# Attention scores as 64-row matmuls in couples on the two halves of TensorE's rows

## The chip, the cores and the metric

The kernel runs on one core of a Trainium2 chip. The metric is the device time of one execution in microseconds, the median of three runs. Five engines work side by side, each through its own queue in order: TensorE (PE in the profile, with its weight loads listed apart as PEld), VectorE (DVE), ScalarE (ACT), GpSimd (POOL) and SyncE (SP, which here only issues DMAs).

## The reference, cut to what matters

Attention with normed queries and keys, then a low-rank mixer and a two-layer MLP:

```python
# q, k, v: (8, 12, 448, 64); U: (448, 32); V: (32, 448); w_ch1: (768, 3072); w_ch2: (3072, 768)
q_n, k_n = rmsnorm(q, g_q), rmsnorm(k, g_k)            # over the 64 values of a head
scores = 0.125 * q_n @ k_n.transpose(0, 1, 3, 2)       # 448 x 448 for each head
attn = softmax(scores) ; a = attn @ v                  # heads side by side: x (8, 448, 768)
u = x + ((x.transpose(0, 2, 1) @ U) @ V).transpose(0, 2, 1)
out = u + np.maximum(u @ w_ch1, 0.0) @ w_ch2
```

A head is 64 wide, half of the 128 rows over which a full matmul of TensorE sums. 448 keys are three and a half blocks of 128.

## The kernel before

**Groups and pairs.** The 96 heads (8 batches of 12) are worked in 48 pairs, six to a batch, and loaded in 24 groups of two pairs. For a pair, `qT` holds 128 rows by 448 tokens: head 0 in rows 0 to 63, head 1 in rows 64 to 127, with the gains multiplied in.

**Keys, `kz`.** For a pair there are 128 rows by 896 columns: the 448 keys of head 0 stand in rows 0 to 63 with zeros below them, then the 448 keys of head 1 in rows 64 to 127 with zeros above them. So each block of 128 columns can be multiplied with all of `qT`, and the zeros drop the wrong head. Seven blocks make up a pair: three of head 0, a shared one with the last 64 keys of both heads, three of head 1. For the first six groups the keys are turned by TensorE (`turn`) and copied into `kz` by VectorE (`take_k`, L359 to L361). From group 6 on (`DMA_FROM`) GpSimd scales them into `kp` (`scale_dma`, L188 and L192), 14 blocks of 128 with the zeros in place, and SyncE's transposing DMAs bring them into `kz` (`turn_dma`, L367 and L369); then GpSimd multiplies the gains into `qT` (`take_dma`, L374).

**Scores, `Sc(b, pr, r)`.** For r = 0 to 2 two matmuls (L398) of 128 x 448 go into the two banks of a tile `sc` (pool `ps_sc`, two tiles), and one exponential on ScalarE (L399) takes both to the tile `E`, 128 x 896. For r = 3 there is one matmul and an exponential half as long.

**Values, `V(b, pr, half)`.** 14 matmuls (L412 and L416) read `E` as weights and write a tile `pv` of the pool `ps`, which has four tiles of one bank each and serves everything else too; two operations of VectorE finish them. The first matmul of each seven reads the block of last keys.

**Mixer and MLP.** For each batch: `mix_t`, `mix_tr`, `mix_rows` (L433, L440, L485), 24 `up` (six matmuls of 128 x 448 at L500, then a Relu on ScalarE, L502), and `down` (L526: units of six matmuls of 128 x 384).

**The order.** It is written out by hand (`manual_schedule`). Two lists are merged by a planner: `att`, the attention steps, each with a cost, and `mlp`, the units of mixer and MLP. A step of `att` is taken as long as its costs so far are not ahead of what is due beside the MLP. Batch 0 runs before the MLP, in an order of its own (`extra`). From batch 1 on, the four `Sc` of a pair are four steps, with the two `V` of the pair before, the turns (`T`), the squares and sums of later groups, and the loads between them. Since attention runs ahead (`LEAD`), it ends well before the MLP does.

Of the kernel before, what the change touches and what calls it, by code (L numbers as in the profile page):

```python
# [9 lines left out]
FP32 = mybir.dt.float32  # L10
BF16 = mybir.dt.bfloat16
# [8 lines left out]
DMA_FROM = 6  # L20
# [4 lines left out]
def kernel(  # L25
# [13 lines left out]
    nc = tc.nc  # L39
# [43 lines left out]
    va_bufs = [consts.tile([P, NM, D1], BF16, name=f"va{i}") for i in range(3)]  # L83
    vl_bufs = [consts.tile([P, 2, 2 * D1], BF16, name=f"vl{i}") for i in range(3)]

    kp = consts.tile([P, 2 * NT, P], BF16)
    q_bufs = [consts.tile([P, 2, S], BF16, name=f"qT{i}") for i in range(2)]
    kz_bufs = [consts.tile([P, 2, 2 * S], BF16, name=f"kz{i}") for i in range(2)]

    def load_qk(gi, i, eng=None):  # L90
        b, h0, n = groups[gi]
# [84 lines left out]
    def scale_dma(gi, i):  # L176

        src = staged[gi][i].rearrange("p (c j) d -> p c j d", c=2)
        rs = rss[gi][:, i].rearrange("p (c j) -> p c j ()", c=2)
        for c in range(2):  # L180
            if i == 0:
                dst = normed[gi][0][:, :, c]
                odd = groups[gi][0] % 2
                main, rest = dst[:, odd:odd + 2 * NJ], dst[:, (1 - odd) * 2 * NJ]
            else:
                dst = normed[gi][1].rearrange("p (c j) (x d) -> p c j x d", c=2, x=2)[:, c, :, c]
                main, rest = dst[:, c:c + 2 * NJ], dst[:, (1 - c) * 2 * NJ]
            nc.gpsimd.tensor_tensor(  # L188
                main.rearrange("p (t i) d -> p i t d", i=2),
                src[:, c, :2 * NJ].rearrange("p (i t) d -> p i t d", i=2),  # L190
                rs[:, c, :2 * NJ].rearrange("p (i t) o -> p i t o", i=2).to_broadcast([P, 2, NJ, D]), ALU.mult)
            nc.gpsimd.tensor_tensor(rest, src[:, c, 2 * NJ], rs[:, c, 2 * NJ].to_broadcast([P, D]), ALU.mult)  # L192
# [49 lines left out]
    for va, vl in zip(va_bufs, vl_bufs):  # L242
        nc.vector.memset(va[:, :, D:D1], 1.0)
        nc.vector.memset(vl, 0.0)
        for e in range(2):
            nc.vector.memset(vl[e * R:(e + 1) * R, :, e * D1 + D:(e + 1) * D1], 1.0)
    for t, eng in zip(kz_bufs, (nc.vector, nc.gpsimd)):
        for a in range(2):
            eng.memset(t[D:P, a, :S], 0.0)
            eng.memset(t[0:D, a, S:], 0.0)  # L250
    for e in range(2):
        nc.gpsimd.tensor_mul(gp[:, e * D:(e + 1) * D], grow[:, 0, :], grow[:, 1, :])

# [101 lines left out]

    def take_k(gi, a):
        src = pts[(gi, 1)][:, :, a, :]
        kz = kz_bufs[gi % 2][:, a]
        nc.vector.tensor_copy(kz[0:D, :S].rearrange("p (j r) -> p j r", r=R), src[0:D])  # L359
        nc.vector.tensor_copy(kz[D:P, S:S + R], src[D:P, 2 * NJ])  # L360
        nc.vector.tensor_copy(kz[D:P, S + R:].rearrange("p (j r) -> p j r", r=R), src[D:P, :2 * NJ])  # L361
        qk[(gi, a)].append(kz)

    def turn_dma(gi):
        for a in range(2):
            rows = slice(a * R, (a + 1) * R)
            nc.sync.dma_start_transpose(q_bufs[gi % 2][:, a].rearrange("p (j r) -> p j r", r=R),  # L367
                                        normed[gi][0][rows].rearrange("p j c d -> p (j c d)"))
            nc.sync.dma_start_transpose(kz_bufs[gi % 2][:, a].rearrange("p (g r) -> p g r", r=R),  # L369
                                        kp[rows].rearrange("p g x -> p (g x)"))  # L370

    def take_dma(gi):
        qT = q_bufs[gi % 2]
        nc.gpsimd.tensor_scalar(qT, qT, gg[:, 0:1], None, ALU.mult)  # L374
        for a in range(2):
            qk[(gi, a)] = [qT[:, a], kz_bufs[gi % 2][:, a]]

    def T(gi, i):
        if gi >= DMA_FROM:
# [8 lines left out]
    NB = 2 * NJ + 1  # L388

    def Sc(b, pr, r):  # L390
        qT, kz = qk[divmod(b * NPAIR + pr, 2)]
        if r == 0:
            es[(b, pr)] = ep.tile([P, NB, S], BF16, name="E", tag="E")
        n = min(2, NB - 2 * r)
        sc = ps_sc.tile([P, 2, 512], FP32, name="sc", tag="sc")
        for i in range(n):
            c = (2 * r + i) * P
            nc.tensor.matmul(sc[:, i, :S], kz[:, c:c + P], qT, start=True, stop=True)  # L398
        nc.scalar.activation(es[(b, pr)][:, 2 * r:2 * r + n, :], sc[:, :n, :S], AF.Exp, scale=scal, bias=bias)  # L399

    def V(b, pr, half):
        if b not in xs:
            xs[b] = xp.tile([P, NW, dm], BF16, name="x", tag="x")
        gi, lp = divmod(b * NPAIR + pr, 2)
        va, vl = normed[gi][2:]
        first_h, step = (2 * lp, 1) if gi == BESIDE else (lp, 2)
        h0 = groups[gi][1] + first_h
        E = es[(b, pr)]
        pv = ps.tile([P, 2, 2, D1], FP32, name="pv", tag="ps")
        for i in range(2):  # L410
            w = WIN[b % 2][2 * half + i]
            nc.tensor.matmul(pv[:, i].rearrange("p e d -> p (e d)"), E[:, NJ, w:w + P], vl[:, lp, :],  # L412
                             start=True, stop=False)
            for e in range(2):
                for j in range(NJ):
                    nc.tensor.matmul(pv[:, i, e, :], E[:, e * (NJ + 1) + j, w:w + P],  # L416
                                     va[:, (first_h + step * e) * NJ + j, :], start=False, stop=(e == 1 and j == NJ - 1))
        r = headp.tile([P, 2, 2], FP32, name="r", tag="r")
        nc.vector.reciprocal(r, pv[:, :, :, D])  # L419
        nc.vector.tensor_tensor(  # L420
            xs[b].rearrange("p i (h d) -> p i h d", d=D)[:, 2 * half:2 * half + 2, h0:h0 + step + 1:step, :],
            pv[:, :, :, :D],
            r.rearrange("p i e -> p i e ()").to_broadcast([P, 2, 2, D]), ALU.mult)
# [124 lines left out]
    def add_att(cost, f, *a):  # L548
        att.append((cost, f, a))
# [55 lines left out]
    for i, (b, pr) in enumerate(pairs):  # L605
        if b == 0:
            continue
        gi, a = divmod(i, 2)
        more = gi + 1 < len(groups)
        by_dma = gi + 1 >= DMA_FROM  # L610
        soon = gi + 2 < len(groups)

        if pr == 0 and b > 1:
            add_att(0.55, V, *pairs[i - 1], 0)
            add_att(0.55, V, *pairs[i - 1], 1)
        add_att(0.38, Sc, b, pr, 0)
        if i == 2 * DMA_FROM - 2:
            add_att(0.0, load, DMA_FROM + 1)
        if a == 0 and by_dma and gi + 1 < len(groups):
            add_att(0.0, scale_all, gi + 1)  # L620
        if b == 1 and pr == 0:
            add_att(0.4, lambda: None)
        if a == 0 and not by_dma:
            add_att(0.0, squares, gi + 1, 0, nc.gpsimd)
            add_att(0.0, squares, gi + 1, 1, nc.gpsimd)
            if gi + 2 >= DMA_FROM:
                add_att(0.0, load, gi + 2)
        add_att(0.38, Sc, b, pr, 1)
        if pr != 0:
            add_att(0.55, V, *pairs[i - 1], 0)  # L630
        if a == 1 and more and not by_dma:
            add_att(0.39, T, gi + 1, 0)
        if a == 1 and soon and gi + 2 >= DMA_FROM:
            add_att(0.0, squares, gi + 2, 0)
            add_att(0.0, squares, gi + 2, 1)
        add_att(0.38, Sc, b, pr, 2)
        if a == 0 and not by_dma:
            add_att(0.0, sums, gi + 1, 0)
            add_att(0.0, sums, gi + 1, 1)
        if a == 0 and more and by_dma:  # L640
            add_att(0.0, turn_dma, gi + 1)
            add_att(0.0, take_dma, gi + 1)
            if gi + 1 == DMA_FROM:
                add_att(0.0, weights, 2)
            if gi + 3 < len(groups):
                add_att(0.0, load, gi + 3)
        if a == 1 and more and not by_dma:
            add_att(0.39, T, gi + 1, 1)
        if a == 0 and not by_dma:
            add_att(0.0, scale_all, gi + 1)  # L650
        add_att(0.19, Sc, b, pr, 3)
        if pr != 0:
            add_att(0.55, V, *pairs[i - 1], 1)
        if a == 1 and soon and gi + 2 >= DMA_FROM:
            add_att(0.0, sums, gi + 2, 0)
            add_att(0.0, sums, gi + 2, 1)
    add_att(0.55, V, *pairs[-1], 0)
    add_att(0.55, V, *pairs[-1], 1)

# [93 lines left out]
    while ia < len(att) or im < len(mlp):  # L753
# [6 lines left out]
        if take_att:  # L760
            c, f, a = att[ia]
            if f is load:
                later.append((f, a))
            else:
                f(*a)
            if ia >= a_from:
                ca += c
            ia += 1
            if f is scale_all:
                weights(2)  # L770
            if f is T and a == (DMA_FROM - 1, 1):
                nc.vector.memset(kp, 0.0)
        else:
            c, f, a, _ = mlp[im]
            f(*a)
            turning = f is mix_t and a[0] > 0 or turning and a != (a[0], NW - 1, 1)
            cm += c
            im += 1
# [30 lines left out]
```

## Time and profile before

| What | Value |
|---|---|
| median of 3 runs (lowest, highest) | 601.6 us (601.02, 602.13) |
| span of the profiled execution | 600.9 us |
| around the span, to the median of the runs | 0.7 us |
| PE busy, share of the span | 585.0 us, 97% |
| ACT busy | 313.5 us, 52% |
| DVE busy / POOL busy | 200.2 us, 33% / 203.3 us, 34% |
| DMA | 71.73 MB, mean 119 GB/s |
| granted TensorE clock | full speed in all 40 slices |
| matmuls of the scores (L398) | 336, 93.9 us busy, mean 352 ns |
| exponentials (L399) | 144 of 896 columns, mean 1003 ns; 48 of 448, mean 635 ns |
| first and last matmul of the scores | 11.3 us, 486.3 us |

Matmuls overlap in the pipeline, so the mean of 352 ns is not what one of them costs in a row of many: twelve matmuls of 448 columns last 2.27 us. The page counts an engine as busy while anything of its is in flight; idle time is put down to the event that ended it. The first 44 us are batch 0, in which TensorE is busy 36.3 us; from 110 us to 470 us it is busy throughout.

### The profile page before, as it was taken

The page shows a single profiled execution, that of the slowest core. Times are in us where ns is not written, and L with a number is a line of the kernel's source. Part 1 is how long each engine was busy: PE and PEld are TensorE (multiplying, and loading weights), DVE is VectorE, ACT ScalarE, POOL GpSimd, SP SyncE. Part 2 cuts the span into 40 slices and gives each one's busy share as a digit, 9 for nine tenths or more (in the row PEclk, how much of TensorE's full clock was granted, in tenths as well). Part 3 has the DMA queues.
Part 4 walks back from the last instruction along what each step waited for, and adds up shares of the span by engine and source line. Part 5 has one row for each costly group of instructions (what it writes and reads, how often), then busy time and mean ns, then how long its engine had stood idle before and what let it go on. Part 6 is the DMA issues. An engine that isn't in the chain of part 4 may idle for free.

```text
span 600.9 us, 11614 instructions
## 1 busy us (share of the span) xinstructions
PE 585.0 (97%) x4791; PEld 356.1 (59%) x4792; DVE 200.2 (33%) x456; ACT 313.5 (52%) x482; POOL 203.3 (34%) x290
## 2 busy tenths in 40 slices
PE   8798999999999999999999999999999999999996
PEld 7464666655666556655566655665566655655563
DVE  6785544512334212531235320531233310310011
ACT  6866793467454776357654567356763344004300
POOL 6996655335054323425144413524233000000000
PEclk9999999999999999999999999999999999999999
DMA  8899999685279451973275742677026310230022
GB/s 224 201 240 239 259 180 215 127 199 100 85 150 161 127 131 32 193 178 82 58 164 100 188 116 41 151 180 169 9 38 100 74 27 0 53 74 1 0 53 52
DMA packets 118332, 71.73 MB, mean 119 GB/s; under 512 B 80392, under 2 KB 115080, under 8 KB 118280
## 3 DMA queue, kind: packets, MB, share of 16 engines
q1 hardware_dynamic: 108868, 61.56, 45.5%
q0 software_dynamic: 9408, 9.44, 9.7%
q8 instruction: 37, 0.61, 0.4%
q14 instruction: 15, 0.12, 0.1%
q10 hardware_dynamic: 4, 0.00, 0.0%
HBM read 52.20 MB, written 11.01 MB: 105 GB/s over the span
## 4 chain that ended last, share of the span: by engine, by line
PE 90%; DMA 4%; DVE 2%; ACT 1%; issue 0%; POOL 0%; SPq 0%; DVEq 0%; ACTq 0%
PE ph L500 36%; PE po L526 34%; PE sc L398 9%; PE pv L416 5%; DMA kz<-kp 2%; PE pv L412 2%; DMA kf<-in_k_dram 2%; PE pm L485 1%; ACT E L399 1%; DMA out_dram<-ob 1%; PE pu L433 1%; DVE ssq L159 1%; PE pt L344 0%; PE sc L512 0%; POOL kp L169 0%
## 5 line engine op out<-in xcount | busy, mean ns | idle before, releaser
L526 PE MATMUL po<-w2b,hT 128*128 128x384 bf16 x1344 | 241.8, 326 | 0.0
L500 PE MATMUL ph<-uT,w1b 128*128 128x448 bf16 x1140 | 234.4, 352 | 0.0
L399 ACT ACTIVATE E<-sc,gg 128x896 bf16<-128x896 f32 x192 | 172.5, 911 | 112.7 <-PE sc L398 112.5
L526 PEld LDWEIGHTS <-hT 128*128 128x128 bf16 x1344 | 126.7, 98 | 78.8
L502 ACT ACTIVATE hT<-ph 128x448 bf16<-128x448 f32 x190 | 102.9, 544 | 121.2 <-PE ph L500 118.9
L500 PEld LDWEIGHTS <-w1b 128*128 128x128 bf16 x1140 | 108.2, 97 | 95.4
L398 PE MATMUL sc<-qT,kz 128*128 128x448 bf16 x336 | 93.9, 352 | 7.7 <-ACT E L399 5.9
L419 DVE RECIPROCAL r<-pv 128x4 f32<-128x4 f32 x96 | 17.4, 181 | 210.7 <-PE pv L416 209.9
L188 POOL TENSOR_TENSOR qn<-qf,rs 128x384 bf16<-128x384 f32 x36 | 29.9, 829 | 152.7 <-ACT rs L166 137.7
L374 POOL TENSOR_SCALAR qT<-qT,gg 128x896 bf16<-128x896 bf16 x18 | 45.4, 2522 | 85.7 <-DMA qT<-qn 64.3
L534 DVE TENSOR_TENSOR ob<-po,x 128x384 f32<-128x384 f32 x48 | 26.8, 558 | 94.8 <-PE po L526 91.1
L416 PE MATMUL pv<-va,E 128*128 128x65 bf16 x1152 | 57.3, 194 | 0.0
L416 PEld LDWEIGHTS <-E 128*128 128x128 bf16 x1152 | 50.6, 98 | 7.7 <-issue 0.3
L398 PEld LDWEIGHTS <-kz 128*128 128x128 bf16 x336 | 31.8, 97 | 32.1 <-issue 7.1
L159 DVE TENSOR_REDUCE ssq<-sq 128x14 f32<-128x896 f32 x45 | 46.8, 1076 | 0.2
L412 PE MATMUL pv<-vl,E 128*128 128x130 bf16 x192 | 42.1, 220 | 0.1
L420 DVE TENSOR_TENSOR x<-pv,r 128x256 bf16<-128x256 f32 x96 | 40.8, 424 | 3.3
L490 DVE TENSOR_TENSOR x<-pm,x 128x384 bf16<-128x384 f32 x48 | 26.3, 553 | 17.4 <-PE pm L485 15.2
L188 POOL TENSOR_TENSOR kp<-kf,rs 128x384 bf16<-128x384 f32 x36 | 29.8, 828 | 0.0
L412 PEld LDWEIGHTS <-E 128*128 128x128 bf16 x192 | 18.7, 97 | 7.6 <-issue 0.6
L196 POOL CAST va<-vf 128x768 bf16<-128x768 f32 x24 | 20.6, 860 | 0.0
L534 DVE TENSOR_TENSOR ob<-po,u_rest 128x384 f32<-128x384 f32 x8 | 4.5, 558 | 45.9 <-PE po L526 45.9
(91 smaller groups left out, 285.6 us busy)
## 6 DMA issues: line engine op xcount, KB each, us to landing
qf<-in_q_dram SPq DMA_DIRECT2D x23, 448.0 KB, 4.1
kf<-in_k_dram SPq DMA_DIRECT2D x23, 448.0 KB, 4.9
out_dram<-ob SPq DMA_DIRECT2D x50, 192.0 KB, 2.9
vf<-in_v_dram SPq DMA_DIRECT2D x48, 192.0 KB, 5.6
w1b<-in_moe_w_ch_dram POOLq DMA_DIRECT2D x4, 1152.0 KB, 18.5
w2b<-in_moe_w_ch_dram POOLq DMA_DIRECT2D x8, 576.0 KB, 15.3
vf<-in_v_dram SPq DMA_DIRECT2D x48, 32.0 KB, 4.6
out_dram<-ob SPq DMA_DIRECT2D x12, 96.0 KB, 3.3
```

Source lines behind the costliest of these rows:

```text
L159: nc.vector.tensor_reduce(ssqs[gi][:, i, :], sqs.pop((gi, i)), AX, ALU.add)
L188: nc.gpsimd.tensor_tensor(main.rearrange("p (t i) d -> p i t d", i=2), src[:, c, :2 * NJ].rearrange("p (i t) d -> p i t d", i=2), rs[:, c, ...
L374: nc.gpsimd.tensor_scalar(qT, qT, gg[:, 0:1], None, ALU.mult)
L398: nc.tensor.matmul(sc[:, i, :S], kz[:, c:c + P], qT, start=True, stop=True)
L399: nc.scalar.activation(es[(b, pr)][:, 2 * r:2 * r + n, :], sc[:, :n, :S], AF.Exp, scale=scal, bias=bias)
L412: nc.tensor.matmul(pv[:, i].rearrange("p e d -> p (e d)"), E[:, NJ, w:w + P], vl[:, lp, :], start=True, stop=False)
L416: nc.tensor.matmul(pv[:, i, e, :], E[:, e * (NJ + 1) + j, w:w + P], va[:, (first_h + step * e) * NJ + j, :], start=False, stop=(e == 1 and ...
L420: nc.vector.tensor_tensor(xs[b].rearrange("p i (h d) -> p i h d", d=D)[:, 2 * half:2 * half + 2, h0:h0 + step + 1:step, :], pv[:, :, :, :D ...
L500: nc.tensor.matmul(ph, w1b[:, dt, ht * P:(ht + 1) * P], uT[:, dt, off:off + S], start=(dt == 0), stop=(dt == KD - 1))
L502: nc.scalar.activation(hT[:, ht, off:off + S], ph, AF.Relu)
L526: nc.tensor.matmul(po, hT[:, ht, col:col + P], w2b[:, ht, half * HALF:(half + 1) * HALF], start=(ht == 0), stop=(ht == KH - 1))
L534: nc.vector.tensor_tensor(ob[:, h], po, urows(b, col, half), ALU.add)
```

## The change

Keys without zeros: `kT` has 128 rows by 512 columns (448 + 64), three blocks that hold head 0's keys in rows 0 to 63 and head 1's in rows 64 to 127, and a fourth block with the last 64 keys of both heads, with zeros where the other head's rows are. For r = 0 to 2 a score step is now a couple: one matmul on rows 0 to 63 for head 0, one on rows 64 to 127 for head 1, each of 64 rows by 128 columns and 448 wide, into the two banks of `sc`. The block of last keys stays one matmul over 128 rows, but from batch 1 on it goes into a one-bank tile `sl` of the pool `ps`.

From batch 1 on, the score steps stand in three stretches for two pairs (`Srows`): (r0, r1) of the first pair; (r2 of the first, r0 of the second, r3 of the first); (r1, r2, r3 of the second). So each stretch has two couples, and the second and third end with a matmul over 128 rows. The costs in the planner's list and the places of `V`, `scale_all`, `turn_dma`, `take_dma`, squares and sums change with them: the first `V` of a group's first pair now follows the second stretch, which ends with that pair's last exponential. Batch 0 keeps its order, with a couple wherever it had two matmuls. `kp` shrinks from 14 blocks to 8, and with it the transposing DMA of the keys; `take_k` copies 128 x 384 once and 64 x 64 twice. `V` reads the same blocks of `E` at other places.

```diff
-    kp = consts.tile([P, 2 * NT, P], BF16)
+    kp = consts.tile([P, NT + 1, P], BF16)
-    kz_bufs = [consts.tile([P, 2, 2 * S], BF16, name=f"kz{i}") for i in range(2)]
+    kT_bufs = [consts.tile([P, 2, S + R], BF16, name=f"kT{i}") for i in range(2)]
...
-        kz = kz_bufs[gi % 2][:, a]
-        nc.vector.tensor_copy(kz[0:D, :S].rearrange("p (j r) -> p j r", r=R), src[0:D])
-        nc.vector.tensor_copy(kz[D:P, S:S + R], src[D:P, 2 * NJ])
-        nc.vector.tensor_copy(kz[D:P, S + R:].rearrange("p (j r) -> p j r", r=R), src[D:P, :2 * NJ])
+        kT = kT_bufs[gi % 2][:, a]
+        nc.vector.tensor_copy(kT[:, :SM].rearrange("p (j r) -> p j r", r=R), src[:, :2 * NJ])
+        for c in range(2):
+            d = slice(c * D, (c + 1) * D)
+            nc.vector.tensor_copy(kT[d, SM + c * R:SM + (c + 1) * R], src[d, 2 * NJ])
...
         n = min(2, NB - 2 * r)
-        sc = ps_sc.tile([P, 2, 512], FP32, name="sc", tag="sc")
+        if r < NJ or b == 0:
+            sc = ps_sc.tile([P, 2, 512], FP32, name="sc", tag="sc")
+        else:
+            sc = ps.tile([P, 1, 512], FP32, name="sl", tag="ps")
+        keys = slice(r * P, (r + 1) * P)
         for i in range(n):
-            c = (2 * r + i) * P
-            nc.tensor.matmul(sc[:, i, :S], kz[:, c:c + P], qT, start=True, stop=True)
+            d = slice(i * D, (i + 1) * D) if r < NJ else slice(0, P)
+            nc.tensor.matmul(sc[:, i, :S], kT[d, keys], qT[d], start=True, stop=True)
         nc.scalar.activation(es[(b, pr)][:, 2 * r:2 * r + n, :], sc[:, :n, :S], AF.Exp, scale=scal, bias=bias)
...
+        nxt = pairs[i + 1 - a]
...
+        if a == 0:
+            add_att(0.5, Srows, ((b, pr, 0), (b, pr, 1)))
...
+            if by_dma and more:
+                add_att(0.0, scale_all, gi + 1)
...
+            if pr != 0:
+                add_att(0.55, V, *pairs[i - 1], 0)
+                add_att(0.55, V, *pairs[i - 1], 1)
+            add_att(0.7, Srows, ((b, pr, 2), (*nxt, 0), (b, pr, 3)))
...
+            if more and by_dma:
+                add_att(0.0, turn_dma, gi + 1)
+                add_att(0.0, take_dma, gi + 1)
...
+            add_att(0.55, V, b, pr, 0)
+        else:
+            add_att(0.7, Srows, ((b, pr, 1), (b, pr, 2), (b, pr, 3)))
...
+            add_att(0.55, V, *pairs[i - 1], 1)
```

More of the change, by code (lines that the diff above doesn't have):

```diff
@@ L185, in scale_dma @@
             else:
-                dst = normed[gi][1].rearrange("p (c j) (x d) -> p c j x d", c=2, x=2)[:, c, :, c]
-                main, rest = dst[:, c:c + 2 * NJ], dst[:, (1 - c) * 2 * NJ]
+                dst = normed[gi][1][:, :, c * D:(c + 1) * D]
+                main, rest = dst[:, :2 * NJ], dst[:, 2 * NJ + c]
             nc.gpsimd.tensor_tensor(
@@ L246 @@
             nc.vector.memset(vl[e * R:(e + 1) * R, :, e * D1 + D:(e + 1) * D1], 1.0)
[L247 to L250, printed above, removed]
+    for t, eng in zip(kT_bufs, (nc.vector, nc.gpsimd)):
+        eng.memset(t[D:P, :, SM:S], 0.0)
+        eng.memset(t[0:D, :, S:], 0.0)
     for e in range(2):
@@ L357, in take_k @@
         src = pts[(gi, 1)][:, :, a, :]
-        kz = kz_bufs[gi % 2][:, a]
-        nc.vector.tensor_copy(kz[0:D, :S].rearrange("p (j r) -> p j r", r=R), src[0:D])
-        nc.vector.tensor_copy(kz[D:P, S:S + R], src[D:P, 2 * NJ])
-        nc.vector.tensor_copy(kz[D:P, S + R:].rearrange("p (j r) -> p j r", r=R), src[D:P, :2 * NJ])
-        qk[(gi, a)].append(kz)
+        kT = kT_bufs[gi % 2][:, a]
[3 more added lines that the diff above has]
+            nc.vector.tensor_copy(kT[d, SM + c * R:SM + (c + 1) * R], src[d, 2 * NJ])
+        qk[(gi, a)].append(kT)
     def turn_dma(gi):
@@ L368, in turn_dma @@
                                         normed[gi][0][rows].rearrange("p j c d -> p (j c d)"))
-            nc.sync.dma_start_transpose(kz_bufs[gi % 2][:, a].rearrange("p (g r) -> p g r", r=R),
+            nc.sync.dma_start_transpose(kT_bufs[gi % 2][:, a].rearrange("p (g r) -> p g r", r=R),
                                         kp[rows].rearrange("p g x -> p (g x)"))
@@ L375, in take_dma @@
         for a in range(2):
-            qk[(gi, a)] = [qT[:, a], kz_bufs[gi % 2][:, a]]
+            qk[(gi, a)] = [qT[:, a], kT_bufs[gi % 2][:, a]]
     def T(gi, i):
@@ L390, in Sc @@
     def Sc(b, pr, r):
-        qT, kz = qk[divmod(b * NPAIR + pr, 2)]
+        qT, kT = qk[divmod(b * NPAIR + pr, 2)]
         if r == 0:
@@ L394, in Sc, with Srows @@
         n = min(2, NB - 2 * r)
-        sc = ps_sc.tile([P, 2, 512], FP32, name="sc", tag="sc")
+        if r < NJ or b == 0:
[3 more added lines that the diff above has]
+        keys = slice(r * P, (r + 1) * P)
         for i in range(n):
-            c = (2 * r + i) * P
-            nc.tensor.matmul(sc[:, i, :S], kz[:, c:c + P], qT, start=True, stop=True)
+            d = slice(i * D, (i + 1) * D) if r < NJ else slice(0, P)
+            nc.tensor.matmul(sc[:, i, :S], kT[d, keys], qT[d], start=True, stop=True)
         nc.scalar.activation(es[(b, pr)][:, 2 * r:2 * r + n, :], sc[:, :n, :S], AF.Exp, scale=scal, bias=bias)
+    def Srows(blocks):
+        for x in blocks:
+            Sc(*x)
     def V(b, pr, half):
@@ L411, in V @@
             w = WIN[b % 2][2 * half + i]
-            nc.tensor.matmul(pv[:, i].rearrange("p e d -> p (e d)"), E[:, NJ, w:w + P], vl[:, lp, :],
+            nc.tensor.matmul(pv[:, i].rearrange("p e d -> p (e d)"), E[:, 2 * NJ, w:w + P], vl[:, lp, :],
                              start=True, stop=False)
@@ L415, in V @@
                 for j in range(NJ):
-                    nc.tensor.matmul(pv[:, i, e, :], E[:, e * (NJ + 1) + j, w:w + P],
+                    nc.tensor.matmul(pv[:, i, e, :], E[:, 2 * j + e, w:w + P],
                                      va[:, (first_h + step * e) * NJ + j, :], start=False, stop=(e == 1 and j == NJ - 1))
@@ L615 @@
             add_att(0.55, V, *pairs[i - 1], 1)
[L616 to L652, printed above, removed]
-            add_att(0.55, V, *pairs[i - 1], 1)
-        if a == 1 and soon and gi + 2 >= DMA_FROM:
-            add_att(0.0, sums, gi + 2, 0)
-            add_att(0.0, sums, gi + 2, 1)
+        if a == 0:
+            add_att(0.5, Srows, ((b, pr, 0), (b, pr, 1)))
+            if i == 2 * DMA_FROM - 2:
+                add_att(0.0, load, DMA_FROM + 1)
+            if by_dma and more:
+                add_att(0.0, scale_all, gi + 1)
+            if b == 1 and pr == 0:
+                add_att(0.4, lambda: None)
+            if not by_dma:
+                add_att(0.0, squares, gi + 1, 0, nc.gpsimd)
+                add_att(0.0, squares, gi + 1, 1, nc.gpsimd)
+                if gi + 2 >= DMA_FROM:
+                    add_att(0.0, load, gi + 2)
+            if pr != 0:
+                add_att(0.55, V, *pairs[i - 1], 0)
+                add_att(0.55, V, *pairs[i - 1], 1)
+            add_att(0.7, Srows, ((b, pr, 2), (*nxt, 0), (b, pr, 3)))
+            if not by_dma:
+                add_att(0.0, sums, gi + 1, 0)
+                add_att(0.0, sums, gi + 1, 1)
+            if more and by_dma:
+                add_att(0.0, turn_dma, gi + 1)
+                add_att(0.0, take_dma, gi + 1)
+                if gi + 1 == DMA_FROM:
+                    add_att(0.0, weights, 2)
+                if gi + 3 < len(groups):
+                    add_att(0.0, load, gi + 3)
+            if not by_dma:
+                add_att(0.0, scale_all, gi + 1)
+            add_att(0.55, V, b, pr, 0)
+        else:
+            add_att(0.7, Srows, ((b, pr, 1), (b, pr, 2), (b, pr, 3)))
+            if more and not by_dma:
+                add_att(0.39, T, gi + 1, 0)
+            if soon and gi + 2 >= DMA_FROM:
+                add_att(0.0, squares, gi + 2, 0)
+                add_att(0.0, squares, gi + 2, 1)
+            add_att(0.55, V, *pairs[i - 1], 1)
+            if more and not by_dma:
+                add_att(0.39, T, gi + 1, 1)
+            if soon and gi + 2 >= DMA_FROM:
+                add_att(0.0, sums, gi + 2, 0)
+                add_att(0.0, sums, gi + 2, 1)
@@ L771 @@
             if f is T and a == (DMA_FROM - 1, 1):
-                nc.vector.memset(kp, 0.0)
+                nc.vector.memset(kp[:, 2 * NJ:], 0.0)
         else:
```

## The prediction, made before the changed kernel ran

> **What bounds the kernel now.** I read the page's totals and chain first, then the waits of TensorE, and then the timeline where I needed a price. All times of the sum are made against the profiled span of 600.9 us; the median of the runs, 601.6 us, lies 0.7 us above it, and I carry that over.
>
> ```profile
> PE 585.0 (97%) x4791; PEld 356.1 (59%) x4792; DVE 200.2 (33%) x456; ACT 313.5 (52%) x482; POOL 203.3 (34%) x290
> ...
> PE 90%; DMA 4%; DVE 2%; ACT 1%; issue 0%; POOL 0%; SPq 0%; DVEq 0%; ACTq 0%
> ```
>
> TensorE is the bound: 97% busy, 90% of the chain that ended last. After 110 us its waits come to nothing, so there a matmul less is time less, and a wait more is time more. What waits it has lie early, and most are for the exponentials that empty `sc`:
>
> ```profile
> PE sc L398 <- ACT E L399: 5.9, 8, 2.1
> ...
> PE sc L398 <- POOL qT L374: 0.8, 1, 0.8
> ```
>
> The columns are the total wait, the number of waits and the longest, in us. The longest, 2.1 us, stands at 53 us in batch 1.
>
> **The gain of a couple.** In the chain, twelve matmuls of 448 columns take 2.27 us, 0.189 us each:
>
> ```profile
> 125.70 2.27 PE ph L500 x12
> ```
>
> Batches 1 to 7 have 42 pairs with three couples each, 126 couples in 63 stretches of two. If the halves work beside each other, a stretch needs 2 x 0.189 us where it needed 4 x 0.189 us: 0.378 us less, 23.8 us for 63.
>
> No row shows two matmuls beside each other. The second of a couple can start when its own weights are in. The nearest row is the one in which each short matmul has its own weight load: six matmuls of 65 columns last 0.35 us, a single one 0.194 us, so they start 0.031 us apart. I take 0.03 us for the lag of the second half, once in a stretch, 1.9 us in all. By the Trainium skill (TensorE: Matmul & The Clock Gate, "The mechanism") packed tiles start about 4 ns apart; by that figure the lag would be 0.3 us in all; no run here shows it yet.
>
> **The price of changing the tile.** A stretch goes from full matmuls to 64-row ones and back: 126 changes. The trace of before has one place where the rows of the tile change, the gains near the start, a 1-row matmul between full ones:
>
> ```profile
> 7.19 0.50 PE L235 MATMUL busy<-ident 128*128 128x128 bf16 x6
> 7.62 0.27 PE L263 MATMUL pg<-ob 1*128 1x1 f32 x1
> ...
> 8.24 0.38 PE L264 MATMUL pg<-ob 1*128 1x1 f32 x2 [0.25 <-DVE ob L261]
> 8.56 0.23 PE L235 MATMUL busy<-ident 128*128 128x128 bf16 x1
> ```
>
> Columns are start, length, engine, line. One `busy` matmul lasts 0.220 us, so six in 0.50 us start 0.056 us apart; the sixth starts at 7.47 us and a seventh would at 7.525 us. The 1-row matmul starts at 7.62 us: 0.094 us lost on the way in. On the way back the second `pg` starts at 8.38 us (0.38 us for two of which one lasts 0.25 us) and the first full one at 8.56 us, 0.178 us later. Two `pg` stand 0.134 us apart, the shortest matmuls 0.031 us, so 0.045 to 0.147 us is lost on the way out; I take the middle, 0.096 us. The load ahead of each first matmul can't be hidden: the second full one follows after 0.066 us in place of 0.055 us, so 0.01 us for each change. Sum: 0.094 + 0.096 + 0.02 = 0.21 us per stretch, 13.2 us for 63. Bounds: the way in had a satisfied wait in its queue, so it may cost nothing, which leaves 0.05 us (3 us); or every change waits for the whole recorded tail, 0.352 - 0.189 = 0.163 us, twice with the loads 0.35 us (22 us).
>
> The Trainium skill says that changing the tiling mode drains TensorE (TensorEngine Tiling (Array Packing), "Key Properties"). This speaks against the change, and the gaps of 0.094 us and more at `pg` agree with it. The Trainium skill does not say there how long a drain is; the upper bound above is the reading in which it is the whole tail.
>
> So TensorE's own time falls by 23.8 - 1.9 - 13.2 = 8.7 us. A couple alone would lose: 0.189 - 0.03 - 0.21 = -0.05 us. Batch 0 has 18 of these, 0.9 us, but TensorE is busy for only 36.3 us of the first 44 us and fills gaps with `busy`, so I count nothing; without that cover it is the 0.9 us.
>
> **New waits.** The score steps are now bunched, and three exponentials follow on each other: in a run of them one starts every 0.91 us (from 55.35 us, two of 896 columns take 1.91 us; one takes 1.00 us), the short one lasts 0.635 us. From the start of a stretch with two couples and last keys the exponentials end after about 0.45 + 0.91 + 0.91 + 0.635 = 2.9 us; the stretch itself takes 0.6 + 0.2 us.
>
> - `V` right after its own stretch. Its first matmul reads the last keys, the last of three exponentials, and on TensorE everything queued behind `V` waits with it. In the changed order of batch 1 the second stretch of each group is followed by a single `up` (1.14 us), with or without one `mix_rows` (0.16 us), then `V`: it comes after 1.9 to 2.1 us, and waits 0.8 to 1.0 us, with a Relu in the queue ahead 1.2 us. Three groups: 3.6 us. In later batches two units (1.95 to 2.27 us) lie between, so it is 0 to 0.2 us: 0.5 us in all.
> - In batch 1 the first two stretches have one `up` between them. Both `sc` tiles are then full until about 2.4 us, and the second couple comes at 1.8 us: 0.7 us.
> - The 2.06 us at 53 us goes. There the exponentials stood behind the roots, which waited 1.68 us for VectorE's sums:
>
> ```profile
> 53.94 0.32 ACT L165 ACTIVATE rs<-ssq,eps 128x28 f32<-128x28 f32 x1 [1.68 <-DVE ssq L159]
> ...
> 55.08 0.54 PE L398 MATMUL sc<-qT,kz 128*128 128x448 bf16 x2 [2.06 <-ACT E L399]
> ```
>
>   In the changed order the roots come behind all of the second stretch, so they hold up Relus and not a full pair of `sc`. What is late next is the 0.7 us above.
> - Queries of the next group. The roots follow the first stretch, so they wait for two exponentials in place of one, 0.9 us more. From there GpSimd's scaling, SyncE's transposes and the gains take 11.3 us (139.27 to 150.58 us for one group), and the scores wait for the last:
>
> ```profile
> 139.04 0.23 ACT L166 ACTIVATE rs<-rs 128x28 f32<-128x28 f32 x1
> ...
> 148.05 2.52 POOL L374 TENSOR_SCALAR qT<-qT,gg 128x896 bf16<-128x896 bf16 x1 [3.17 <-DMA qT<-qn]
> ```
>
>   In the first of these groups there is no slack (gains end at 97.01 us, the scores start at 97.06 us), 0.5 us in the second, 2.6 us in the third; most later ones have over 3 us. I count 1.5 us for the first two. The keys' transpose shrinks from 14 blocks to 8, but of 1.23 us that it holds the queue for little can come off, as the queries' with 7 blocks holds it for 1.22 us.
>
> Sum of the waits: 3.6 + 0.5 + 0.7 - 2.06 + 1.5 = 4.2 us.
>
> **What is free.** VectorE's copies of keys (378 + 194 + 353 ns for a pair before, about 353 + 2 x 194 ns after) and the smaller clearing of `kp` (0.8 us before) lie beside TensorE's work; only 0.9 us of waits on `kz` in batch 0 could move. Reading `E` at other places changes no count. `sl` holds one of four tiles of `ps` for some 2.9 us; an `up` that comes round to it is 3.4 us later, so I count nothing, and up to 0.6 us each in batch 1 if a `V` lies between.
>
> **The sum:** 601.6 - 8.7 + 4.2 = 597.1 us.
>
> **Rivals.**
> - *The whole tail at each change* (slower). Two changes cost 0.35 us, a stretch then gains 0.378 - 0.03 - 0.35 = 0, and the waits stay: about 606 us. It decides from the point where two changes cost over (23.8 - 1.9 - 4.2) / 63 = 0.28 us. For it: my way out is the middle of a wide range, and 1-row matmuls may drain sooner. Against: the way in was measured at 0.094 us. Chance 0.19.
> - *Cheap changes.* With 0.05 to 0.14 us per stretch TensorE gains 13 to 19 us, 587 to 593 us. For it: the wait queued ahead of `pg`. Chance 0.13.
> - *Queries late in each batch.* The group after a batch's first has the shortest window, 17.0 us (scores at 163.56 and 180.60 us) with 2.6 us of slack. By the planner's costs that window falls from 3.76 of 14.58 to 3.0 of 12.3 of a batch, about 1 us, and the roots come 0.9 us later: 0.8 us is left. If that is gone too and 1.5 us is waited in seven batches, it is 607 us. Chance 0.08.
> - *The halves do not work beside each other.* Then the 23.8 us stay and the changes are paid: 619 to 621 us. Nothing in the trace shows packing either way. Chance 0.05.
>
> **The numbers.** The forecast, 0.14 to 0.28 us per stretch, holds 0.55 and spans 592 to 601.6 us; 0.09 of it, and 0.02 of the first rival, lie within 0.2% of before, about what runs of this kernel can tell from no change. So faster 0.13 + 0.46 = 0.59, same 0.11, slower 0.17 + 0.08 + 0.05 = 0.30. The range, 590 to 607 us, takes in the first rival and the dearer half of the second, and leaves out cheaper changes and serial halves.
>
> **What would show it.** Right: the second matmul of a couple starts 0.01 to 0.06 us after the first; couples 0.19 us apart; gaps of some 0.1 us around each stretch; `V` waiting about 1 us for `E` three times before 90 us; no new waits of TensorE beyond 5 us in sum after 44 us. Wrong: couples 0.38 us apart; gaps of 0.17 us or more; or scores waiting for `qT` once in each batch.

## The result, and the profile after

The changed kernel took 597.86 us (median of five runs, 596.07 to 599.84), the kernel before beside it 602.08 us: a ratio of 0.9935, 95% interval 0.9914 to 0.9955, or 2.7 to 5.2 us less. Forecast were 597.1 us. The profiled execution is the shortest of the five, 596.07 us with a span of 594.3 us, so its difference to the profile of before, 6.6 us, is more than that of the medians.

The totals and the chain of the page, changed kernel:

```profile
PE 574.3 (97%) x4792; PEld 333.5 (56%) x4792; DVE 196.5 (33%) x454; ACT 307.4 (52%) x482; POOL 201.9 (34%) x288
...
PE 90%; DMA 3%; ACT 3%; POOL 1%; DVE 1%; SPq 1%; issue 1%; POOLq 0%; ACTq 0%
```

TensorE still is the bound, with less to do. Its timeline at one stretch with last keys, in a batch without waits (start, length, engine, line):

```profile
300.30 2.11 PE L534 MATMUL po<-w2b,hT 128*128 128x384 bf16 x12
302.35 0.55 PE L402 MATMUL sc<-qT,kT 64*128 64x448 bf16 x4
302.83 0.36 PE L402 MATMUL sl<-qT,kT 128*128 128x448 bf16 x1
303.03 3.09 PE L534 MATMUL po<-w2b,hT 128*128 128x384 bf16 x18
```

The twelve `po` of 0.162 us each end their streams at 302.25 us, and the first couple starts 0.10 us later. Four matmuls are done with in 0.55 us, of which 0.35 us is the length of one: the second couple starts 0.20 us behind the first. A further 0.19 us on, 0.09 us pass before `sl`. In single records of the trace 59 of the 63 stretches look the same: 0.095 us on the way in, 0.003 us between the halves, 0.200 us from couple to couple, 0.094 us on the way out, and 0.012 us more than its own length for the full matmul behind (here 0.200 us instead of 0.188 us). The other four stand at waits, at 50, 61, 94 and 114 us. So a stretch takes 0.095 + 0.200 + 0.003 + 0.188 + 0.094 + 0.012 = 0.592 us, where four full matmuls took 0.756 us: 0.164 us less, 10.3 us for 63.

The waits of TensorE, and where they stand in its timeline (the wait in brackets):

```profile
PE sc L402 <- ACT E L403: 3.8, 8, 0.9
PE sc L402 <- POOL qT L374: 3.2, 2, 1.8
PE pv L420 <- ACT E L403: 2.7, 3, 1.0
```

```profile
50.28 0.36 PE L402 MATMUL sc<-qT,kT 64*128 64x448 bf16 x2 [0.41 <-ACT E L403]
53.03 0.23 PE L420 MATMUL pv<-vl,E 128*128 128x130 bf16 x1 [0.80 <-ACT E L403]
...
69.23 0.23 PE L420 MATMUL pv<-vl,E 128*128 128x130 bf16 x1 [0.88 <-ACT E L403]
...
84.41 0.23 PE L420 MATMUL pv<-vl,E 128*128 128x130 bf16 x1 [1.04 <-ACT E L403]
...
94.01 0.56 PE L402 MATMUL sc<-qT,kT 64*128 64x448 bf16 x4 [1.80 <-POOL qT L374]
...
114.33 0.56 PE L402 MATMUL sc<-qT,kT 64*128 64x448 bf16 x4 [1.42 <-POOL qT L374]
```

With two waits more (0.45 us for `kT` at 61 us, 0.73 us for `tb` at 376 us) they come to 7.5 us after the first 44 us, where before there were 2.06 + 0.82 = 2.9 us. The first `up`, with which the MLP begins behind batch 0, before and after:

```profile
43.08 1.30 PE L500 MATMUL ph<-uT,w1b 128*128 128x448 bf16 x6
```

```profile
42.04 1.30 PE L508 MATMUL ph<-uT,w1b 128*128 128x448 bf16 x6
```

The account of the spans: -10.3 us in the stretches, +4.6 us of waits, -1.0 us in batch 0: -6.7 us for the measured -6.6 us. It is an account of the two profiled executions. The median run of the changed kernel is 1.8 us longer than its profiled one, and no profile shows where.

### The profile page after: what moved, and what is told of

It reads as the page before. It is cut to its first block, busy times and chain, and to the rows that moved or that the text cites. A ratio compares the mean times of both kernels' runs of the same rounds, so it can differ in the third digit from the quotient of the medians.

```text
span 594.3 us, 11608 instructions
## 1 busy us (share of the span) xinstructions
PE 574.3 (97%) x4792; PEld 333.5 (56%) x4792; DVE 196.5 (33%) x454; ACT 307.4 (52%) x482; POOL 201.9 (34%) x288
## 4 chain that ended last, share of the span: by engine, by line
PE 90%; DMA 3%; ACT 3%; POOL 1%; DVE 1%; SPq 1%; issue 1%; POOLq 0%; ACTq 0%
PE ph L508 36%; PE po L534 36%; PE pv L424 6%; PE sc L402 5%; ACT E L403 2%; PE sl L402 2%; PE pv L420 2%; PE pm L493 2%; DMA qT<-qn 1%; DMA vf<-in_v_dram 1%; POOL qT L374 1%; PE pt L343 1%; PE pu L441 1%; DVE ssq L159 1%; ACT hT L510 0%
## 5 line engine op out<-in xcount | busy, mean ns | idle before, releaser
L534 PE MATMUL po<-w2b,hT 128*128 128x384 bf16 x1344 | 238.0, 326 | 0.0
L508 PE MATMUL ph<-uT,w1b 128*128 128x448 bf16 x1140 | 229.4, 352 | 0.0
L403 ACT ACTIVATE E<-sc,gg 128x896 bf16<-128x896 f32 (+1 forms) x150 | 140.3, 990 | 120.6 <-PE sc L402 120.4
L402 PE MATMUL sc<-qT,kT 64*128 64x448 bf16 (+1 forms) x294 | 43.9, 356 | 7.9 <-ACT E L403 3.8
L402 PEld LDWEIGHTS <-kT 64*128 64x128 bf16 (+1 forms) x336 | 14.1, 94 | 46.1 <-issue 42.6
L403 ACT ACTIVATE E<-sl,gg 128x448 bf16<-128x448 f32 x42 | 26.9, 639 | 0.0
```

Source lines behind the costliest of these rows:

```text
L402: nc.tensor.matmul(sc[:, i, :S], kT[d, keys], qT[d], start=True, stop=True)
L508: nc.tensor.matmul(ph, w1b[:, dt, ht * P:(ht + 1) * P], uT[:, dt, off:off + S], start=(dt == 0), stop=(dt == KD - 1))
L534: nc.tensor.matmul(po, hT[:, ht, col:col + P], w2b[:, ht, half * HALF:(half + 1) * HALF], start=(ht == 0), stop=(ht == KH - 1))
```

## The experiments

Two theories stood against each other: the couples bring the gain and the new order costs some of it; or the gain comes from the order, or from the shorter transposes and copies of keys, and the couples only pay for their changes. Kernels of one group ran on one chip beside their own runs of the kernel before; the ratios compare across groups.

### The changed kernel again

> The changed kernel as it is, beside the others on the same chip. Theory: 63 stretches of 0.164 us less each are 10.3 us of TensorE's time; batch 1 and the first queries turned by DMA give back some 4 to 5 us in waits. Expected 596 to 600 us, about 4 to 6 us under the kernel before. If the time varies from run to run by the wait for the queries, it varies more than that of the kernel before.

596.76 us against 602.19 us, ratio 0.9913 (0.9896 to 0.9930). The same gaps, and 3.7 us of waits for `qT`. The time did not vary more than that of the kernel before: its five runs lie within 1.3 us, the 21 of the kernel before within 3.3 us.

### The order without the couples

```diff
-            d = slice(i * D, (i + 1) * D) if r < NJ else slice(0, P)
-            nc.tensor.matmul(sc[:, i, :S], kT[d, keys], qT[d], start=True, stop=True)
+            c = (r + i * (NJ + 1) if r < NJ else NJ) * P
+            nc.tensor.matmul(sc[:, i, :S], kz[:, c:c + P], qT, start=True, stop=True)
```

`kz`, `kp`, `take_k` and the transposes are those of the kernel before. The costs in the planner's list stay those of the changed kernel, so this order is not tuned for full matmuls.

> The new order of steps (three stretches for two pairs, last keys in the one-bank tile, V at its new places), but with keys padded by zeros and full 128-row matmuls as before. Theory (the couples bring the gain, the order costs): no couples and no changes of the tile, so only the new waits are left: 3 to 5 us slower than before, about 605 us, with V of batch 1 waiting for E three times by about 1 us. Rival (the gain is the order's, which no longer holds up ScalarE at 53 us, or comes with it): as fast as the changed kernel or at least faster than before, 598 to 601 us.

611.82 us against 602.19 us, ratio 1.0175 (1.0142 to 1.0208): 9.6 us slower than before by the medians, twice what was expected, and the rival is out. `V` waited as expected (0.73, 0.71 and 0.87 us). What had been sized too small were the queries. The timeline of TensorE, and its windows (times of the window; busy time of PE, PEld, DVE, ACT, POOL; then the granted clock, DMA share and GB/s):

```profile
98.29 1.65 PE L401 MATMUL sc<-qT,kz 128*128 128x448 bf16 x4 [4.08 <-POOL qT L374]
...
122.12 0.92 PE L401 MATMUL sc<-qT,kz 128*128 128x448 bf16 x4 [1.90 <-POOL qT L374]
```

```profile
92.00:96.00 4.00, 2.21 (x25) 1.40 (x24) 3.17 (x7) 0.41 (x1) 0.29 (x1) 1.00 1.32 186
96.00:100.00 4.00, 1.71 (x5) 0.71 (x5) 0.00 (x0) 0.71 (x1) 2.24 (x1) 0.56 1.35 150
100.00:104.00 4.00, 4.00 (x16) 2.00 (x15) 0.00 (x0) 1.63 (x4) 2.26 (x5) 0.59 1.08 291
```

In the wait of 4.08 us, which ends at 98.29 us, and behind it the granted clock was 0.56 and 0.59 over two windows of four us: the same four matmuls took 1.65 us at 98 us and 0.92 us at 122 us. All waits after 44 us are 9.5 us, 6.6 us more than before, and the low clock behind the wait takes about 2.5 us more. So the order alone is a loss; what is gained comes with the 64-row keys.

### The couples in the old order

The loop over the pairs is that of the kernel before, with last keys in `sc`.

> The old order with the 64-row couples one at a time between other matmuls, last keys in the tile sc as before. Theory: a couple alone takes 0.095 + 0.012 + 0.188 + 0.004 + 0.094 + 0.012 = 0.405 us in place of 0.378 us, so 126 of them cost 3.4 us and nothing else moves: 605 us, less where two couples happen to stand together. Rival (the shorter transposes and copies of the keys give the gain): 597 to 600 us, as they are all kept here.

603.72 us, ratio 1.0022 (1.0010 to 1.0033): slower, by 1.3 us (by the ratio) and not by 3.4 us. The rival's 597 to 600 us is out. A couple alone in the timeline:

```profile
300.22 2.12 PE L534 MATMUL po<-w2b,hT 128*128 128x384 bf16 x12
302.28 0.36 PE L402 MATMUL sc<-qT,kT 64*128 64x448 bf16 x2
302.57 1.15 PE L534 MATMUL po<-w2b,hT 128*128 128x384 bf16 x6
```

From the end of the `po` streams (300.22 + 0.01 + 12 x 0.162 = 302.17 us, the 0.01 us for the open first load) to the next `po` there are 0.40 us, where two full matmuls take 0.38 us. From batch 2 to batch 6 this kernel lost 0.3 to 0.5 us a batch, as the price of a lone couple says (18 times 0.025 us); but its profile won 1.9 us in batch 0, and did not wait for `qT` at all. That profile is of the shortest of its twelve runs, and its span, 600.0 us, is 0.9 us below that of the profile of before. The two shortest runs had a mean granted clock of 0.999, the ten longer ones 0.993 to 0.996, so a part of the 1.3 us can be the clock. That the shorter transposes and copies give a part back is likely, but no run here has them alone.

### Two changes of the tile more for each stretch

```diff
-            add_att(0.7, Srows, ((b, pr, 2), (*nxt, 0), (b, pr, 3)))
+            add_att(0.7, Srows, ((b, pr, 2), (b, pr, 3), (*nxt, 0)))
...
-            add_att(0.7, Srows, ((b, pr, 1), (b, pr, 2), (b, pr, 3)))
+            add_att(0.7, Srows, ((b, pr, 1), (b, pr, 3), (b, pr, 2)))
```

> The changed kernel with one edit: in the 42 stretches with last keys, the full matmul stands between the two couples and not behind them, so each of these has two more changes of the tile. Theory (each pair of changes costs 0.213 us with its two open loads): 42 x 0.213 = 8.9 us slower than the changed kernel, less up to 2 us because V of the first pair finds its last exponential earlier: 604 to 607 us. Rival (the gaps at the changes are only the first matmul waiting for something else, or are hidden): within 2 us of the changed kernel.

The edit gives 42 of the 63 stretches two changes more. 605.84 us, ratio 1.0061 (1.0039 to 1.0084), in the same group as the changed kernel with 596.76 us: 9.1 us slower, where the theory had 8.9 us less up to 2 us. One of its stretches:

```profile
303.23 0.36 PE L402 MATMUL sc<-qT,kT 64*128 64x448 bf16 x2
303.52 0.36 PE L402 MATMUL sl<-qT,kT 128*128 128x448 bf16 x1
303.82 0.36 PE L402 MATMUL sc<-qT,kT 64*128 64x448 bf16 x2
304.11 3.10 PE L534 MATMUL po<-w2b,hT 128*128 128x384 bf16 x18
```

0.29 us from the couple to `sl`, 0.30 us from `sl` to the next couple, 0.29 us to the `po`: each of the three steps carries its change of about 0.1 us, which nothing hides. In single records such a stretch lasts 0.982 us from the end of the stream before it to the next matmul, and 0.779 us in the changed kernel; with the open load behind it, 0.012 us, that is 0.215 us, 9.0 us for 42. Its three waits of `V` for `E` were gone, and its waits for `qT` had grown to 5.3 us, once 3.8 us.

That the medians differ by 9.1 us, so close to 8.9 us, is in part luck, since the granted clock was low here too. The windows of this run (columns as above):

```profile
92.00:96.00 4.00, 1.54 (x7) 0.47 (x7) 0.00 (x0) 0.89 (x1) 2.41 (x1) 0.67 1.22 171
96.00:100.00 4.00, 4.00 (x14) 1.92 (x13) 0.00 (x0) 1.45 (x4) 2.44 (x5) 0.50 1.15 292
```

TensorE waited for queries until 94.46 us; from there to 100.2 us half the clock is missing, 2.9 us. The profiled span is 605.1 us, 10.8 us above the changed kernel's: 9.0 us of changes, 2.9 us of low clock, and 0.8 us less of waits, 11.1 us in all. The ten runs spread from 602.41 us at a mean clock of 1.000 to 609.71 us at 0.985.

### The queries' transposes first

```diff
         for a in range(2):
             rows = slice(a * R, (a + 1) * R)
             nc.sync.dma_start_transpose(q_bufs[gi % 2][:, a].rearrange("p (j r) -> p j r", r=R),
                                         normed[gi][0][rows].rearrange("p j c d -> p (j c d)"))
+        for a in range(2):
+            rows = slice(a * R, (a + 1) * R)
             nc.sync.dma_start_transpose(kT_bufs[gi % 2][:, a].rearrange("p (g r) -> p g r", r=R),
```

> The changed kernel with one edit: the two transposes of the queries stand ahead of the two of the keys on SyncE, so the second one of the queries no longer waits for the scaled keys (2.1 us at group 9). Theory (the first two groups of queries turned by DMA come late, 3.2 to 3.7 us of waits, and this wait differs from run to run): gains end 2 us earlier or more, 3 to 4 us faster than the changed kernel, 593 to 594 us, and no wait for qT in the trace. Rival (the queries are bound elsewhere, by the crowded DMA engines at 85 to 95 us or by the keys, which now come later): within 1 us of the changed kernel, with scores waiting for kT in place of qT.

593.22 us against 601.49 us, ratio 0.9857 (0.9829 to 0.9885). SyncE's timeline for group 6, first in the changed kernel, then here:

```profile
82.13 1.32 SPq L367 DMA_TRANSPOSE qT<-qn  x1
84.20 1.20 SPq L369 DMA_TRANSPOSE kT<-kp  x1
85.50 1.20 SPq L367 DMA_TRANSPOSE qT<-qn  x1
```

```profile
81.73 2.67 SPq L367 DMA_TRANSPOSE qT<-qn  x2
84.51 2.52 SPq L371 DMA_TRANSPOSE kT<-kp  x2
```

The second transpose of the queries is issued with the first and no longer behind one that waits for scaled keys. Of the waits for `qT` 0.4 us is left, once:

```profile
111.03 0.55 PE L404 MATMUL sc<-qT,kT 64*128 64x448 bf16 x4 [0.39 <-POOL qT L376]
```

The runs spread from 592.82 to 594.33 us, 1.5 us; those of the changed kernel spread over 3.8 us in the first group but 1.3 us in the second, so a smaller spread is not shown.

### `V` of batch 1 moved behind the next stretch

```diff
-            add_att(0.55, V, b, pr, 0)
+            if b > 1:
+                add_att(0.55, V, b, pr, 0)
+            else:
+                add_att(0.55, lambda: None)
         else:
...
+            if b == 1:
+                add_att(0.0, V, *pairs[i - 1], 0)
             add_att(0.55, V, *pairs[i - 1], 1)
```

> The changed kernel with one edit: in batch 1 the first V of each group's first pair moves from right behind its own stretch to behind the next stretch and the first turn, and an empty step of the same cost holds its place in the plan. Theory of the prediction (these three waits for E cost what they measure): 2.7 us less, 594 us. Rival (batch 1 is bound by GpSimd's scaling ahead of the turns, and a wait taken away comes back there): no gain, within 0.5 us of the changed kernel, with waits for qn or kp at the turns of about 1.2 us each.

598.0 us, ratio 0.9947 (0.9924 to 0.9969): no gain. The rival held:

```profile
55.71 0.56 PE L343 MATMUL pt<-ident,qn 128*128 128x128 bf16 x7 [0.66 <-POOL qn L169]
...
71.82 0.56 PE L343 MATMUL pt<-ident,qn 128*128 128x128 bf16 x7 [0.96 <-POOL qn L169]
...
94.00 0.60 PE L402 MATMUL sc<-qT,kT 64*128 64x448 bf16 x4 [3.47 <-POOL qT L374]
```

The waits for `E` are gone (2.7 us); 1.6 us came back at the turns, for GpSimd's scaling, and 1.7 us more are waited for the queries at 94 us. Behind that wait the granted clock was at half from 94.4 to 97.8 us, which takes 1.7 us more, so the next run, without a low clock, is the cleaner one.

### Both

> Both edits. If each wait counts by itself: 6 us under the changed kernel, 591 us. If only the queries' wait counts: as with the queries' transposes first alone, 593 to 594 us. If neither counts: 597 us.

593.50 us, ratio 0.9858 (0.9830 to 0.9885), as with the queries alone: here too 1.6 us are waited at the turns, and 0.72 us in a `mix_rows` at 103 us, together 2.3 us for the 2.7 us taken away.

### The order without couples, with the queries first

> The new order with zero-padded keys and full matmuls, which took 611.8 us and waited 6.0 us for qT, once for so long (4.1 us) that the granted clock fell to 0.56 in the 4 us behind it; now with the queries' transposes ahead of the keys'. Theory (the order costs because the first queries come late): 6 us of waits and 1 to 2 us of half clock go, 604 to 605 us. Rival (the order costs through other things, V and sc): 609 us or more.

605.68 us, ratio 1.0062 (1.0040 to 1.0085): 6.1 us less than without the edit (6.8 us by the ratios), 0.25 us of waits for `qT` in place of 6.0 us, and a full clock. The runs lie within 1.1 us; without the edit they spread over 7.0 us. The order costs 4.2 us still, for `V`, for `sc` and for a `mix_rows`. Between this kernel and the changed one with the same edit there are 12.5 us, which is what 64-row keys bring in this order and with its costs: 10.3 us by the stretches, 1.1 us by the first `up` that comes earlier in these two profiles, and a rest, in which one more wait for a `mix_rows` (1.8 us) stands.

### The edit by itself, and fillers for the clock

The queries first once more, and the same edit in the kernel before:

> The changed kernel with the queries' transposes first, once more, as the neighbour of the two others: 593 to 594 us.

> The kernel before with the queries' transposes first and nothing else. Theory (that edit helps only where queries are late, and before they were late by 0.8 us once): 0 to 1 us faster, 600.6 to 601.6 us, so that the rest of the 8 us between before and the changed kernel with this edit belongs to the couples and their order. Rival (the edit is worth 3 us for any order): 598 to 599 us.

594.12 us, ratio 0.9858 (0.9840 to 0.9876), and 603.48 us, ratio 1.0006 (0.9984 to 1.0029). In the old order the edit gives nothing; queries were late there once by 0.8 us. That wait is gone from the profile, but 0.9 us are waited in a `mix_rows` at 107 us instead.

```diff
-        (2, 1): scales(2) + [(0, weights, (1,)), V2(1, 0)],
-        (2, 3): [V2(1, 1), (0, prep_u, ())],
+        (2, 1): scales(2) + [(0, weights, (1,)), V2(1, 0), (0, keep_busy, (8,))],
+        (2, 2): [(0, keep_busy, (8,))],
+        (2, 3): [V2(1, 1), (0, prep_u, ()), (0, keep_busy, (12,))],
```

> The changed kernel with the queries' transposes first, and 28 more filler matmuls where TensorE waits for exponentials in batch 0 (21 to 24 us), because the granted clock fell to half for 3.4 us behind those waits (25.2 to 28.6 us). Theory (batch 0 is bound by the exponentials and not by TensorE, so the low clock is hidden): clock full in all slices, time unchanged within 0.5 us, 593 to 594 us. Rival (the low clock costs its share of TensorE's time): 1.5 us faster, below 592 us.

593.63 us, ratio 0.9856 (0.9838 to 0.9874): the time of its neighbour. But the neighbour without fillers did not show the low slice in its profile either, so the fillers' part in the clock stays open. Two profiled runs of one kernel, with the low slice (`q_first`, 592.83 us, batch 0 ends at 41.63 us) and without it (`q_first_again`, 594.16 us, 42.76 us), show no loss by it there.

## Why the prediction was right

**The sum.** The mechanism was right: two halves beside each other, a price for each change of the tile, and waits early on. The number is closer than its terms. From the span of before the sum gives 596.4 us, and the profile has 594.3 us: 1.6 us more won in the stretches, 1.0 us in batch 0, 0.4 us more waits. That the median comes within 0.8 us is partly luck, as it lies 1.8 us above the profiled run.

**The couples.** Twice 0.189 us for four matmuls held to 0.012 us, the open load of the second couple. That the halves work beside each other was assumed, with no row for it; the starts 0.003 us apart show it, and `order_only_q_first` against `q_first` with 12.5 us.

**The lag.** 0.03 us was the spacing of short matmuls with a load each. It measured 0.003 us, below the 0.01 to 0.06 us that the prediction gave as a sign of being right: this term of 1.9 us should have been 0.2 us, the largest error of TensorE's sum, which came out at 10.3 us in place of 8.7 us. The Trainium skill's figure (TensorE: Matmul & The Clock Gate, "The mechanism"), about 4 ns, agrees with the trace.

**The changes.** 0.094 us in and 0.096 us out were read from one place of the profile; 0.095 and 0.094 us were measured, and the stretches of `last_between` show that they cost their full length. That the way out fits to 0.002 us is luck: it was the middle of 0.045 to 0.147 us, read from 1-row matmuls. The rival of the whole tail (0.163 us) is out, and so are cheap changes. The Trainium skill names a drain at a change of the tiling mode (TensorEngine Tiling (Array Packing), "Key Properties"). The gaps of 0.095 and 0.094 us agree with it. Weighed together, 0.21 us for two changes and 0.19 us won by a couple, it decides the design: a lone couple loses, as the rows of `couples_alone` show, two win 0.164 us.

**The waits.** 4.2 us were forecast net, 4.6 us measured in the profile, but the terms moved. `V` for `E`: 3.6 us forecast, 2.7 us seen, and none of the 0.5 us in later batches. The 2.06 us at 53 us went as forecast, and 0.4 us stood in its place for the forecast 0.7 us (0.6 us by the prediction's own 2.4 and 1.8 us). Not forecast were 0.45 us for `kT` and 0.73 us for `tb`. The queries: 1.5 us more forecast, 2.4 us more measured (3.2 us in place of 0.8 us). This step was mis-sized in two ways. It took the slack of the first two groups (0.05 and 0.46 us) less the later roots, and left out that TensorE gets there sooner: in the changed kernel it was ready for the first of these groups at 92.21 us and not at 96.24 us, while the gains ended only 3.0 us sooner, so what it gains up to then is in part waited out. And it took the queue of transposes as fixed, when the second transpose of the queries stood behind keys that it does not need. The rival in which queries are late in each batch did not come: from the third group on the slack was 0.5 us or more. It stood nearer than the prediction had it, with 2.6 us as the least slack behind a batch's first group: in batch 6 the profile of before has 0.50 us (gains end at 378.56 us, scores start at 379.06 us).

**Terms that don't add.** The prediction counted the waits for `E` as time. `v_behind` and, without a low clock, `v_behind_q_first` show that they were cover for other waits: taken away, most of them came back at the turns, in a `mix_rows` and at the queries. That the sum of the waits was nearly right while its parts were not is luck. The queries are also what made the order alone so dear: 9.6 us, of which 4.2 us are left with their transposes first. That GpSimd's scaling is what binds all of batch 1 was not tried by making it faster.

**Batch 0** was counted at nothing; it won 1.0 us in the profile. One kernel varies as much there: `q_first` ends batch 0 at 41.63 us and `q_first_again` at 42.76 us. Over all profiles it ends at 41.17 to 42.76 us with 64-row keys (nine) and at 42.55 to 43.08 us without (four). So a gain of some 0.8 us on the average goes with the 64-row keys, and no single pair of profiles shows it; which of copies, transposes and matmuls it is was not tried.

The version that beats both kernels is the changed one with the queries' transposes first: 0.9857 and 0.9858 of the time before, in two groups.

## What to carry to other kernels

Packing two half-height matmuls saves the length of one, but going to the half tile and back costs about 0.21 us here: count how many packed couples stand together, and bunch them before packing. Bunched work fills the queue of the engine behind it and brings the next input's due time forward; look at the slack of what is prepared for the next group before the gain is booked. A wait in the trace is a cost only if what waits behind it is ready sooner. A long wait can also cost the clock: `order_only`, `last_between` and `v_behind` lost 1.7 to 2.9 us more behind waits of 3.5 to 4.1 us.

## What was not expected of the hardware

The loads of weights for the second couple did not hold it up, though both couples use the same rows. All four loads of the stretch at 302 us stand together:

```profile
302.34 0.11 PEld L402 LDWEIGHTS <-kT 64*128 64x128 bf16 x4 [0.32 <-issue]
```

They are through at 302.45 us, while the streams of the first couple end at about 302.53 us, and the second couple follows at 0.200 us (0.188 us at 94 and 114 us, behind the waits for queries). So the next weights of a half load while that half is streaming. And in the profiled run of the changed kernel the granted clock fell to half in batch 0, after waits of 0.37, 0.53 and 0.89 us between 21 and 24 us (TensorE was busy for 1.29 of these 3 us). Windows of 1 us (columns as above):

```profile
24.00:25.00 1.00, 0.84 (x12) 0.37 (x12) 0.83 (x2) 1.00 (x2) 1.00 (x2) 1.00 1.00 174
25.00:26.00 1.00, 1.00 (x15) 0.53 (x12) 1.00 (x1) 1.00 (x2) 1.00 (x1) 0.55 1.09 204
26.00:27.00 1.00, 1.00 (x13) 1.00 (x12) 0.97 (x4) 1.00 (x2) 1.00 (x2) 0.50 1.10 214
27.00:28.00 1.00, 1.00 (x10) 0.77 (x9) 1.00 (x5) 0.12 (x1) 0.98 (x2) 0.50 1.14 221
28.00:29.00 1.00, 1.00 (x16) 0.75 (x15) 0.52 (x4) 0.64 (x1) 1.00 (x2) 0.74 1.12 227
```

The missing shares, 0.45 + 0.50 + 0.50 + 0.26, are 1.7 us, so the clock was at half for 3.4 us. The Trainium skill (TensorE: Matmul & The Clock Gate, "What's actually happening") gives a window of 3.4 us in which the gate watches how busy TensorE is, and half rate as its other state; both agree with these rows. No loss by it shows in batch 0.
